# Retention and a gated MLP on one core: the first eight rows in whole chunks of 128 tokens, and loads that wait for the fourth in front

## The chip, the cores and the metric

The kernel runs on one core of a Trainium2 chip. The metric is device time in microseconds (us), as the median of several executions. A profile is one execution recorded by the hardware: it lists what TensorE (PE, with its weight loads as PEld), VectorE (DVE), ScalarE (ACT), GpSimd (POOL) and SyncE's DMA queue (SP) did, and when.

## What is computed

```python
def _attn_ref(q, k, v):                       # 4 batches, 8 heads, 768 tokens, 64 dims
    gamma = 1.0 - 2.0 ** (-5.0 - np.arange(H))
    for t in range(S):
        state = gamma * state + k[t] outer v[t]
        y[t] = q[t] @ state / sqrt(D)

def _moe_ref(x, w_in, w_out):                 # 3072 x 512, 512 x 2048, 2048 x 512
    h = x @ w_in
    g = h * clip(h + 3, 0, 6) / 6
    return g @ w_out
```

The retention's output, its heads side by side, is the x of the MLP. The weights come as 64-bit floats.

## The kernel before

**Rows and units.** A row is 128 tokens of one batch with all eight heads; there are 24. Row r is chunk n = r // 4 of batch r % 4, so four rows are the same chunk of the four batches. They make a unit of 512 tokens, of which there are six; `UR` is 4.

**Retention of a row.** The recurrence is worked in chunks. Before, each row is cut into two chunks of 64 tokens (c = 0 and 1). `decay` (L448) scales v by ScalarE (four heads) and GpSimd (four) in rows 0 to 3, by ScalarE alone in rows 4 to 7, by GpSimd alone later. `scores` (L361) multiplies k and q of each chunk, in 16 matmuls of 64x64 for the eight heads; `gather` (L385) multiplies k and v, which gives what the chunk adds to the state (16 more). VectorE masks the scores (`fading`, L499, into the tile am). `add_up` (L516) adds to the state of the chunk before: twice a row, on VectorE, or on ScalarE as a copy where there is no state yet. `outer_part` (L348) multiplies q with the state in front of the chunk, and `inner_part` (L373) v with the masked scores; both add in PSUM to y. VectorE scales y into xr (L572), and `split_step` (L241) makes a high part of it on ScalarE and the rest on VectorE: the tile x. `pace` (L343) is a tiny matmul that touches a bank of its own.

**The MLP.** `mm1_step` (L593) makes one h tile: 128 of the 2048 columns for the 512 tokens of a unit, 12 matmuls of 128x512 (L601), since x and w are each in two parts. ScalarE and VectorE make g from h, and SP stores it. `convert` (L182) makes 32-bit weights of a 64-bit tile: one load of 512 KB into one of two staging buffers (st), one step on ScalarE (wm), four on VectorE (wm, wb, wb, ww), and then the split. The second product (L787) runs when all of g is stored, in 1008 matmuls.

**What sets the order.** The program is written as steps, each with an engine, a cost, what it needs and a rank. `Plan.order` (L71) plays them through: TensorE's steps in the order of the code, the others by readiness and rank; the result is the order of each engine's instructions, which is then fixed. Only the numbers in `Plan` decide it; on the chip, each instruction waits for its semaphores in that order. Loads by SP are steps too. The table `FIRST` (L403) fixes the order of the first loads: vn of row 0, the first weight tile, kt, qt, kn, then vn, kt, qt, kn row by row with the tables dq and weight tiles between. All 32 loads of rows 0 to 7 go to the tiles "early". Later rows load into kt, qt, vn and kn; the plan lets such a load start after the third last h tile in the order of the code (L432). Loads are issued on eight semaphores in turn, so that each waits for the eighth DMA in front. Where the plan sees TensorE idle in its first 60 us, `spin` (L700) puts matmuls on constant data, whose results are not used.

Of the kernel before, what the change touches and what calls it, by code (L numbers as in the profile page):

```python
# [19 lines left out]
P = 128  # L20
# [21 lines left out]
class Plan:  # L42
# [3 lines left out]
    FIRST, RATE, FLIGHT = 2.0, 0.00266, 2.0  # L46
# [24 lines left out]
    def order(self):  # L71


        left = {}
        for n, step in enumerate(self.steps):
            step.n = n
            left.setdefault(step.engine, []).append(step)
        for step in self.steps:
            step.all = self.needs(step)
        free = dict.fromkeys(left, self.FIRST)  # L80
        dma = port = self.FIRST
        done = []
        while any(left.values()):
            best = None
            for engine, steps in left.items():
                ready = []
                line = steps[:1] if engine == "PE" else steps
                if engine == "SP" and min(x.rank for x in steps) < -50:
                    line = [min(steps, key=lambda x: x.rank)]
                for step in line:  # L90
                    if all(d.end is not None for d in step.all):
                        at = max([free[engine], port * step.port] + [d.end for d in step.all])
                        ready.append((at, step.rank, step.n, step))
                if ready:
                    t = min(ready)[0]
                    pick = min((r for r in ready if r[0] <= t + 1e-9), key=lambda r: r[1:3])
                    if best is None or t < best[0]:
                        best = (t, pick[3])
            t, step = best
            step.start, free[step.engine] = t, t + step.cost  # L100
            step.end = t + step.cost + step.seen
            if step.port:
                port = t + step.cost
            if step.kb:
                dma = max(dma, t + self.FLIGHT) + step.kb * self.RATE
                step.end = dma
            left[step.engine].remove(step)
            done.append(step)
        return sorted(done, key=lambda x: (x.start, x.n))
# [3 lines left out]
def retention_ffn(ctx: ExitStack, tc: tile.TileContext, qkv, w_in, w_out, dvs, dqs, out, B, H, S, D):  # L113
# [18 lines left out]
    SPIN, FILL = 60.0, 0.7  # L132
    AHEAD = 2 * UR
# [47 lines left out]

    def convert(src, rank, soon=None):  # L182
# [4 lines left out]
        def fetch():  # L187
            t["st"] = wst_tile("st", I64, 2)
            nc.sync.dma_start(out=t["st"], in_=src)
            words = t["st"].bitcast(I32).rearrange("p (n w) -> p n w", w=2)  # L190
            t["lo"], t["hi"] = words[:, :, 0], words[:, :, 1]
# [156 lines left out]
    def outer_part(t, n, states):  # L348

        for i, c, a, h in tiles:  # L350
            if n or c:
                nc.tensor.matmul(  # L352
                    t["y"][halves[a], h, i, cut[c]],
                    states[c][halves[h], a, i],
                    t["qt"]["t"][halves[h], 2 * i + a, cut[c]],
                    start=(i, c) == (0, int(not n)),
                    stop=False,
                    skip_group_check=True,
                )

    def scores(t):  # L361

        for i, c, a, h in tiles:
            nc.tensor.matmul(  # L364
                t["sc"][a][halves[h ^ a], i, c],
                t["kt"]["t"][halves[h], 2 * i + a, cut[c]],
                t["qt"]["t"][halves[h], 2 * i + a, cut[c]],
                start=True,
                stop=True,
                skip_group_check=True,  # L370
            )

    def inner_part(t):  # L373

        for i, c, a, h in tiles:
            nc.tensor.matmul(  # L376
                t["y"][halves[a], h, i, cut[c]],
                t["vn"]["t"][halves[h ^ a], 2 * i + a, cut[c]],
                t["am"][halves[h ^ a], a, i, c],
                start=False,  # L380
                stop=True,
                skip_group_check=True,
            )

    def gather(t, n):  # L385

        for i, c, a, h in tiles:
            if not c or n < ROWS_B - 1:
                nc.tensor.matmul(  # L389
                    t["u"][a][halves[h], c, i],  # L390
                    t["kn"]["t"][halves[h ^ a], 2 * i + a, cut[c]],
                    t["vn"]["t"][halves[h ^ a], 2 * i + a, cut[c]],
                    start=True,
                    stop=True,
                    skip_group_check=True,
                )
# [17 lines left out]
    def load_part(x, src, o, rank):  # L414
# [10 lines left out]
        def fetch():  # L425
# [4 lines left out]
            nc.sync.dma_start(out=to["t"].rearrange("p h n -> p (h n)"), in_=src)  # L430

        return to, box, add("SP", 0.35, fetch, tiles_done[-3:-2], rank, (box,), kb=256)  # L432

    def load(r, rank):
# [13 lines left out]
        def decay(pool, hs):  # L448
# [4 lines left out]
            else:  # L453
# [9 lines left out]
                rank + 3.5,  # L463
                (t["box", "vn"],),
            )
            for pool, hs, size in (((0, slice(0, 4), 4), (1, slice(4, 8), 4)) if r < UR else ((0, slice(0, 4), 4), (0, slice(4, 8), 4)) if r < AHEAD else ((1, slice(0, 8), 8),))
        ]

    def scores_step(r, at):
        t = rows[r]  # L470

        spare = r < UR and r % 2
        t["sc box"] = [plan.box("h", NH) for _ in range(2)] if spare else [plan.box("sc", 1)]

        def run():
# [5 lines left out]
            parts = [b.rearrange("p (b i c n) -> p b i c n", b=2, i=2, n=HALF) for b in banks]  # L481
            t["sc"], t["u"] = ([p[:, b] for p in parts] for b in range(2))
            t["banks"] = [(both, slice(0, 2))] if not spare else [(b[:, None], slice(a, a + 1)) for a, b in enumerate(banks)]
            scores(t)

        t["S"] = add("PE", 0.5, run, (t["got", "kt"], t["got", "qt"]), at, (*t["sc box"], t["box", "kt"], t["box", "qt"]))

    def gather_step(r, at):
        t, n = rows[r], r // UR
# [3 lines left out]
            lambda: gather(t, n),  # L493
# [4 lines left out]

        def fading():  # L499
            t["am"] = apool.tile([P, 2, 2, 2, HALF], F32, tag="am", name=nm("am"), bufs=1)  # L500
            for b, a in t["banks"]:
                nc.vector.tensor_tensor(
                    out=t["am"][:, a].rearrange("p a i c n -> p a (i c) n"),
                    in0=b[:, :, 0 : 2 * P].rearrange("p a (x n) -> p a x n", n=HALF),
                    in1=mask[:, None, None].to_broadcast([P, a.stop - a.start, 4, HALF]),
                    op=ALU.mult,
# [4 lines left out]
        t["A"] = add("DVE", 0.61 + more, fading, (t["S"], t["G"], t["masked"]), at + 2, (*t["sc box"], t["am box"]))  # L511
        t["adds"] = {}
        for c in range(2 if n < ROWS_B - 1 else 1):
            t["state box", c] = plan.box(f"state{c}", 2 + c * (UR - 1))

            def add_up(c=c):  # L516
                new = apool.tile([P, 2, 2, D], F32, tag=f"state{c}", name=nm("state"), bufs=2 + c * (UR - 1))
                was = rows[r - UR]["state", 1] if not c and n else t.get(("state", 0))
                for b, a in t["banks"]:
                    u = b[:, :, (2 + c) * P : (3 + c) * P]  # L520
                    to = new[:, a].rearrange("p a i n -> p a (i n)")
                    if n or c:
                        nc.vector.tensor_tensor(  # L523
                            out=to, in0=u, in1=was[:, a].rearrange("p a i n -> p a (i n)"), op=ALU.add
                        )
                    else:
                        nc.scalar.activation(out=to, in_=u, func=AF.Copy)
                t["state", c] = new
# [3 lines left out]
            if c:  # L532
                boxes.append(t["state box", 0])
                deps.append(t["adds"][0])
            elif n:
                boxes.append(rows[r - UR]["state box", 1])
                deps.append(rows[r - UR]["adds"][1])
            eng = ("DVE", 0.34 + more) if n or c else ("ACT", 0.37 + more)
            t["adds"][c] = add(*eng, add_up, deps, at + 1.5 + 2 * c, boxes)

    def outer_step(r, at):
        t, n = rows[r], r // UR
        t["y box"] = plan.box("y", 1)
        was = rows[r - UR] if n else None

        def run():
            ys = ps_a.tile([P, 2, UT], F32, tag="y", name=nm("y"))[:, :, 0 : 2 * P]
            t["ys"], t["y"] = ys, ys.rearrange("p h (i n) -> p h i n", i=2)
            outer_part(t, n, [was and was["state", 1], t["state", 0]])
            pace()  # L550

        states = [t["state box", 0]] + ([was["state box", 1]] if n else [])
        deps = [t["adds"][0], t["S"], was and was["adds"][1]]
        t["T"] = add("PE", 0.55 if n else 0.3, run, deps, at, (t["y box"], t["box", "qt"], *states))

    def inner_step(r, at):
        t, u = rows[r], r // UR
        n = u

        def run():  # L560
            pace()
            inner_part(t)

        t["I"] = add("PE", 0.55, run, (t["A"], t["T"]), at, (t["y box"], t["am box"], t["box", "vn"]))
# [64 lines left out]
    rows.update((r, {"masked": got_mask}) for r in range(NROW))  # L629
# [41 lines left out]
    for n, (u, jj) in enumerate(turns):  # L671
        while n_w1 < min(NF, jj + 2):
            build_w1(n_w1, next(at) + (0.5 if n_w1 == 0 else 2.0))
# [274 lines left out]
```

## Time and profile before

| | us |
|---|---|
| median of 3 runs (589.95 to 590.63) | 589.98 |
| the profiled execution | 588.12 |
| its span, first to last instruction | 586.3 |
| TensorE busy in the span | 569.6 |
| VectorE busy | 420.2 |
| ScalarE busy | 242.0 |

The profiled execution is 1.86 us below the median of the runs. The span opens with rows 0 to 3, goes on with h tiles between rows, and ends with the second product. Two things are to be kept in mind. Spins count as busy time of PE, and so do matmuls that wait in the pipe. And "issue" in the chain or among the waits is time in which an engine waited for nothing that the profile shows.

### The profile page before, as it was taken

The page shows a single profiled execution, that of the slowest core. Times are in us where ns is not written, and L with a number is a line of the kernel's source. Part 1 is how long each engine was busy: PE and PEld are TensorE (multiplying, and loading weights), DVE is VectorE, ACT ScalarE, POOL GpSimd, SP SyncE. Part 2 cuts the span into 40 slices and gives each one's busy share as a digit, 9 for nine tenths or more (in the row PEclk, how much of TensorE's full clock was granted, in tenths as well). Part 3 has the DMA queues.
Part 4 walks back from the last instruction along what each step waited for, and adds up shares of the span by engine and source line. Part 5 has one row for each costly group of instructions (what it writes and reads, how often), then busy time and mean ns, then how long its engine had stood idle before and what let it go on. Part 6 is the DMA issues. An engine that isn't in the chain of part 4 may idle for free.

```text
span 586.3 us, 13047 instructions
## 1 busy us (share of the span) xinstructions
PE 569.6 (97%) x5250; PEld 467.5 (80%) x5250; DVE 420.2 (72%) x762; ACT 242.0 (41%) x432; POOL 20.2 (3%) x25
## 2 busy tenths in 40 slices
PE   7699999999999999999999999999999999999997
PEld 6577888887888887888888888888888888888885
DVE  4388898998944696443345967998699966899653
ACT  5374444554422343222243544444444344354340
POOL 1000000000000100000000000000000000000000
PEclk9799999999999999999999999999999999999999
DMA  9855756866655566444445529974789536896002
GB/s 328 324 181 202 248 189 231 261 213 221 214 206 173 186 227 210 159 167 146 148 162 189 185 90 340 391 228 119 248 283 315 175 99 190 286 331 208 0 2 107
DMA packets 61260, 119.93 MB, mean 205 GB/s; under 512 B 7056, under 2 KB 7312, under 8 KB 61200
## 3 DMA queue, kind: packets, MB, share of 16 engines
q1 hardware_dynamic: 60912, 119.04, 60.2%
q8 instruction: 41, 0.67, 0.5%
q14 instruction: 19, 0.16, 0.1%
q10 hardware_dynamic: 288, 0.06, 0.0%
HBM read 87.61 MB, written 31.46 MB: 203 GB/s over the span
## 4 chain that ended last, share of the span: by engine, by line
PE 90%; DMA 4%; issue 2%; DVE 1%; POOL 1%; SPq 0%; ACT 0%; DVEq 0%; POOLq 0%
PE h L601 42%; PE o L787 40%; DMA vn<-in_qkv 3%; PE y L376 3%; PE sc L389 2%; PE sc L364 2%; DMA early<-in_qkv 2%; PE y L352 2%; POOL vn L452 1%; SPq L430 0%; DVE x L160 0%; DVE xr L572 0%; DVE w L160 0%; PE spin L703 0%; PE pace L346 0%
## 5 line engine op out<-in xcount | busy, mean ns | idle before, releaser
L601 PE MATMUL h<-x,w 128*128 128x512 f32 x1152 | 268.7, 392 | 1.5 <-DVE x L160 0.9
L601 PEld LDWEIGHTS h<-x,w 128*128 128x128 f32 x1152 | 214.5, 188 | 47.8 <-DVE x L160 1.3
L787 PE MATMUL o<-gc,w 128*128 128x512 f32 x1008 | 233.2, 393 | 0.0
L787 PEld LDWEIGHTS o<-gc,w 128*128 128x128 f32 x1008 | 189.3, 188 | 43.7
L610 DVE SCALAR_TENSOR_TENSOR g<-g,h 128x512 f32<-128x512 f32 x96 | 65.9, 686 | 84.1 <-ACT g L607 83.4
L607 ACT ACTIVATE g<-h,three 128x512 f32<-128x512 f32 x96 | 66.1, 688 | 131.1 <-PE h L601 130.7
L238 ACT ACTIVATE gc<-gr 128x512 fp32r<-128x512 f32 x120 | 71.4, 623 | 56.9 <-PE o L787 43.1
L160 DVE TENSOR_TENSOR gc<-gr,gc 128x512 fp32r<-128x512 f32 x120 | 79.4, 685 | 20.7 <-ACT gc L238 20.7
L238 ACT ACTIVATE gc<-keep 128x512 fp32r<-128x512 f32 x48 | 30.4, 632 | 64.5 <-PE o L787 42.2
L160 DVE TENSOR_TENSOR gc<-keep,gc 128x512 fp32r<-128x512 f32 x48 | 32.9, 687 | 14.0 <-ACT gc L238 13.9
L195 ACT ACTIVATE wm<-st 128x512 f32<-128x512 f32 x32 | 21.5, 671 | 22.7 <-DMA st<-in_w_out 12.5
L246 ACT ACTIVATE x<-xr 128x512 fp32r<-128x512 f32 x24 | 15.1, 629 | 32.4 <-DVE xr L572 32.3
L452 POOL TENSOR_TENSOR vn<-vn,cst_sb 128x512 f32<-128x512 f32 x16 | 17.4, 1090 | 253.0 <-DMA vn<-in_qkv 239.3
L804 DVE SCALAR_TENSOR_TENSOR u<-o,u 128x512 f32<-128x512 f32 (+1 forms) x31 | 20.1, 666 | 6.4 <-PE o L787 6.4
L220 DVE SCALAR_TENSOR_TENSOR ww<-st,wb 128x512 int32<-128x512 int32 x32 | 22.7, 710 | 0.4
L214 DVE SCALAR_TENSOR_TENSOR wb<-st,wb 128x512 int32<-128x512 int32 x32 | 22.0, 686 | 0.3
L160 DVE TENSOR_TENSOR w<-ww,w 128x384 fp32r<-128x384 f32 (+2 forms) x34 | 19.9, 591 | 1.1 <-ACT w L246 1.1
L246 ACT ACTIVATE w<-ww 128x384 fp32r<-128x384 f32 (+2 forms) x34 | 18.5, 550 | 4.6 <-DVE ww L220 4.5
L163 DVE TENSOR_TENSOR keep<-gr,gr 128x512 f32<-128x512 f32 x24 | 16.4, 688 | 4.8 <-DMA gr<-gd 4.5
L523 DVE TENSOR_TENSOR state<-sc,state 128x256 f32<-128x256 f32 (+1 forms) x42 | 16.9, 406 | 4.0 <-PE sc L389 3.7
L199 DVE TENSOR_SCALAR wm<-wm 128x512 f32<-128x512 f32 x32 | 13.5, 422 | 8.3 <-ACT wm L195 8.3
L160 DVE TENSOR_TENSOR x<-xr,x 128x512 fp32r<-128x512 f32 x24 | 16.4, 685 | 1.6 <-ACT x L246 0.9
(51 smaller groups left out, 340.6 us busy)
## 6 DMA issues: line engine op xcount, KB each, us to landing
gr<-gd SPq DMA_DIRECT2D x168, 256.0 KB, 4.1
gd<-g SPq DMA_DIRECT2D x96, 256.0 KB, 3.0
early<-in_qkv SPq DMA_DIRECT2D x32, 256.0 KB, 5.4
st<-in_w_in SPq DMA_DIRECT2D x16, 512.0 KB, 4.0
st<-in_w_out SPq DMA_DIRECT2D x16, 512.0 KB, 3.9
kt<-in_qkv SPq DMA_DIRECT2D x16, 256.0 KB, 3.3
qt<-in_qkv SPq DMA_DIRECT2D x16, 256.0 KB, 3.8
vn<-in_qkv SPq DMA_DIRECT2D x16, 256.0 KB, 4.4
```

The costliest lines, as they stand in the source:

```text
L160: return nc.vector.tensor_tensor(out=out_, in0=a, in1=b, op=ALU.subtract)
L195: nc.scalar.activation(out=t["m"], in_=t["hi"].bitcast(F32), func=AF.Abs)
L214: nc.vector.scalar_tensor_tensor(out=b, in0=t["hi"], scalar=-0x40000000, in1=b, op0=ALU.bitwise_and, op1=ALU.bitwise_or)
L220: nc.vector.scalar_tensor_tensor(out=t["w"].bitcast(I32), in0=t["lo"], scalar=29, in1=t["b"], op0=ALU.logical_shift_right, op1=ALU.bitwise_or,
L238: nc.scalar.activation(out=hi, in_=src, func=AF.Copy)
L246: nc.scalar.activation(out=hi, in_=src, func=AF.Copy)
L452: nc.gpsimd.tensor_tensor(out=v, in0=v, in1=scale[:, :, None].to_broadcast([P, hs.stop - hs.start, D]), op=ALU.mult)
L601: nc.tensor.matmul(h, w[:, o, a], xs[u][b][:, k], start=k + n == 0, stop=(k, n) == (NK - 1, 2), skip_group_check=True)
L607: nc.scalar.activation(out=t["g"], in_=t["h"], func=AF.Relu, bias=three)
L610: ins = nc.vector.scalar_tensor_tensor(out=t["g"], in0=t["g"], scalar=6.0, in1=t["h"], op0=ALU.min, op1=ALU.mult)
L787: nc.tensor.matmul(banks[b, i, h], w2c[jj][:, RIGHT[i], a, h], gc[:, q, c], start=jj == 0 and n == 0, stop=jj == NFP - 1 and n == 2, skip_ ...
L804: nc.vector.scalar_tensor_tensor(out=out_[:, cut], in0=banks[b, i, h][:, cut], scalar=f, in1=other[:, cut], op0=ALU.mult, op1=ALU.add)
```

## The change

**Whole chunks.** The first eight rows (`wide`, r < 8) are one chunk of 128 tokens. Of the 128x128 scores of a head three blocks of 64x64 are needed: two on the diagonal, and one with the keys of the first half and the queries of the second. Scores and inner part take the first half of the keys against all 128 queries (a matmul of 64x128) and the second half against its own (64x64). VectorE still masks the two diagonal blocks; the block off the diagonal is copied to am by ScalarE (`passing`). The two halves of k and v add up in PSUM, so that a row has one state, added once. The outer part takes 128 queries at once against one state, and rows 0 to 3 have none. Rows 8 to 23 stay in chunks of 64.

```diff
-    def outer_part(t, n, states):
+    def outer_part(t, n, states, wide):
         for i, c, a, h in tiles:
-            if n or c:
+            if (n or c) and not (c and wide):
                 nc.tensor.matmul(
-                    t["y"][halves[a], h, i, cut[c]],
+                    t["y"][halves[a], h, i, whole_or_cut(c, wide)],
...
     def gather(t, n, wide):
...
-                    start=True,
-                    stop=True,
+                    start=not wide or (i, c) == (0, 0),
+                    stop=not wide or c == 1,
...
+        def passing():
+            am = am_tile()
+            for b, a in t["banks"]:
+                nc.scalar.activation(
+                    out=am[:, a, :, HALF:P],
+                    in_=b.rearrange("p a (i x n) -> p a i x n", i=2, n=HALF)[:, :, :, 1],
+                    func=AF.Copy,
+                )
...
+        if wide:
+            t["A"].append(add("ACT", 0.37 + more, passing, deps, at + 2, (*t["sc box"], t["am box"])))
...
         for c in range(2 if n < ROWS_B - 1 else 1):
+            if wide and not c:
+                continue
```

**Loads.** Every load of q, k, v, dq and of weights goes through one function that adds a wait for the fourth such load in front; the plan has the same rule. Loads of later rows may be planned two h tiles sooner. The third and fourth weight tiles stand one row earlier in the table of first loads.

```diff
+    def load_from(to, src):
+        ins = nc.sync.dma_start(out=to, in_=src).ins
+        if len(started) >= plan.DEPTH:
+            tc.add_manual_dep(ins, started[-plan.DEPTH], behind, reason="few loads at a time")
+        started.append(ins.name)
...
-        FIRST += {1: [(0, "dq")], 3: [("w", 1)], 4: [(1, "dq")], 5: [("w", 2)], 6: [("w", 3)], 7: [("w", 4)]}.get(r, [])
+    BEHIND = {1: [(0, "dq")], 3: [("w", 1)], 4: [(1, "dq"), ("w", 2)], 5: [("w", 3)], 7: [("w", 4)]}
...
-        return to, box, add("SP", 0.35, fetch, tiles_done[-3:-2], rank, (box,), kb=256)
+        return to, box, add("SP", 0.35, fetch, tiles_done[-5:-4], rank, (box,), kb=256)
```

`FADE`, `W_FIRST`, `W_NEXT` name ranks; FADE is 4.5 where it was 3.5, so the plan takes decays a little later. The first eight rows share out the decays as before.

**What it does to the order.** TensorE, the third row (r = 2). sc is the PSUM tile of its scores and gathered state, y that of the row in front; the tiles early hold the loads. Before:

```order
L364 MATMUL sc_296<-early_125 64x64 x16
L352 MATMUL y_317<-early_118,state_279 64x64 x8
L346 MATMUL pace_326<-mask 64x4
L389 MATMUL sc_296<-early_125 64x64 x16
L346 MATMUL pace_344<-mask 64x4
L376 MATMUL y_317<-am_291,early_125 64x64 x16
```

After, at the same place:

```order
L383 MATMUL sc_267<-early_130 64x128 x4
L383 MATMUL sc_267<-early_130 64x64 x4
L383 MATMUL sc_267<-early_130 64x128 x4
L383 MATMUL sc_267<-early_130 64x64 x4
L408 MATMUL sc_267<-early_130 64x64 x16
L395 MATMUL y_305<-am_262,early_130 64x128 x4
L395 MATMUL y_305<-am_262,early_130 64x64 x4
```

The outer part and both pace matmuls are gone; half of the scores' matmuls, and of the inner part's, are 128 columns wide.

SP's queue from the second dq table on, with what each load waits for (DMAHW is the semaphore of a DMA in front; st is a weight tile). Before:

```order
L430 DMA early_143<-in_decays_y 128x512 [waits DMAHW1_49]
L430 DMA early_200<-in_qkv 128x512 [waits DMAHW2_49]
L430 DMA early_200<-in_qkv 128x512 [waits DMAHW3_49]
L430 DMA early_200<-in_qkv 128x512 [waits DMAHW4_49]
L430 DMA early_200<-in_qkv 128x512 [waits DMAHW5_49]
L189 DMA st_282<-in_w_in 128x512 [waits DMAHW6_49,DVE_49,Activation_49]
```

After:

```order
L189 DMA early_257<-in_decays_y 128x512 [waits DMAHW5_49]
L189 DMA st_411<-in_w_in 128x512 [waits DMAHW6_49,DVE_49,Activation_49]
L189 DMA early_400<-in_qkv 128x512 [waits DMAHW7_49]
L189 DMA early_400<-in_qkv 128x512 [waits DMAHW0_49]
L189 DMA early_400<-in_qkv 128x512 [waits DMAHW1_49]
L189 DMA early_400<-in_qkv 128x512 [waits DMAHW2_49]
L189 DMA st_461<-in_w_in 128x512 [waits DMAHW3_49,DVE_49,Activation_49]
```

The third weight tile moved from behind the four loads of row 5 to ahead of them, and the fourth to right behind them; the semaphores stand for the fourth load in front instead of the eighth.

VectorE, from the masks of the fourth row (am) to the end of its x; wm, wb and ww are steps of the second weight tile. Before:

```order
L502 TENSOR_TENSOR am_449<-sc_374,mask 128x256
L523 TENSOR_TENSOR state_467<-sc_373,state_442 128x128
L523 TENSOR_TENSOR state_467<-sc_374,state_442 128x128
L199 TENSOR_SCALAR wm_445<-wm_445 128x512
L572 TENSOR_TENSOR xr_495<-y_456,early_143 128x512
L160 TENSOR_TENSOR x_294<-xr_447,x_294 128x4x128
L203 TENSOR_SCALAR wb_503<-wm_445 128x512
L214 SCALAR_TENSOR_TENSOR wb_503<-st_186,wb_503 128x512
L160 TENSOR_TENSOR x_294<-xr_495,x_294 128x4x128
```

After:

```order
L542 TENSOR_TENSOR am_404<-sc_335,mask 128x2x2x64
L214 TENSOR_SCALAR wm_398<-wm_398 128x512
L165 TENSOR_TENSOR x_265<-xr_402,x_265 128x4x128
L218 TENSOR_SCALAR wb_442<-wm_398 128x512
L633 TENSOR_TENSOR xr_449<-y_414,early_257 128x512
L229 SCALAR_TENSOR_TENSOR wb_442<-st_327,wb_442 128x512
L235 SCALAR_TENSOR_TENSOR ww_454<-st_327,wb_442 128x512
L165 TENSOR_TENSOR x_265<-xr_449,x_265 128x4x128
```

The additions of the state are gone, and two steps of the weight tile stand between the fourth row's xr and the end of its x, where before there stood a short and a long one, and the x of the third row.

More of the change, by code (lines that the diff above doesn't have):

```diff
@@ L91, in order @@
                     if all(d.end is not None for d in step.all):
-                        at = max([free[engine], port * step.port] + [d.end for d in step.all])
+                        at = max([landed[-self.DEPTH]] if step.kb and len(landed) >= self.DEPTH else [0.0])
+                        at = max([at, free[engine], port * step.port] + [d.end for d in step.all])
                         ready.append((at, step.rank, step.n, step))
@@ L359, in outer_part, with scores @@
                 )
-    def scores(t):
+    def scores(t, wide):
         for i, c, a, h in tiles:
             nc.tensor.matmul(
-                t["sc"][a][halves[h ^ a], i, c],
+                t["sc"](a, i, c)[halves[h ^ a]],
                 t["kt"]["t"][halves[h], 2 * i + a, cut[c]],
-                t["qt"]["t"][halves[h], 2 * i + a, cut[c]],
+                t["qt"]["t"][halves[h], 2 * i + a, whole_or_cut(c, wide)],
                 start=True,
@@ L371, in scores, with inner_part @@
             )
-    def inner_part(t):
+    def inner_part(t, n, wide):
         for i, c, a, h in tiles:
             nc.tensor.matmul(
-                t["y"][halves[a], h, i, cut[c]],
+                t["y"][halves[a], h, i, whole_or_cut(c, wide)],
                 t["vn"]["t"][halves[h ^ a], 2 * i + a, cut[c]],
-                t["am"][halves[h ^ a], a, i, c],
-                start=False,
+                t["masked"](a, i, c)[halves[h ^ a]],
+                start=wide and not n and (i, c) == (0, 0),
                 stop=True,
@@ L383, in inner_part, with gather @@
             )
-    def gather(t, n):
+    def gather(t, n, wide):
         for i, c, a, h in tiles:
@@ L470, in scores_step @@
         t = rows[r]
-        spare = r < UR and r % 2
+        spare, wide = r < UR and r % 2, r < AHEAD
         t["sc box"] = [plan.box("h", NH) for _ in range(2)] if spare else [plan.box("sc", 1)]
@@ L492, in gather_step @@
             0.5 if n < ROWS_B - 1 else 0.25,
-            lambda: gather(t, n),
+            lambda: gather(t, n, wide),
             (*t["faded"], t["got", "kn"]),
@@ L531, in gather_step @@
             deps = [t["G"]]
[L532 to L538, printed above, removed]
+            if before:
+                boxes.append(before["state box", k])
+                deps.append(before["adds"][k])
+            eng = ("ACT", 0.37 + more) if first_ else ("DVE", 0.34 + more)
@@ L539, in gather_step, with y_tile @@
             t["adds"][c] = add(*eng, add_up, deps, at + 1.5 + 2 * c, boxes)
+    def y_tile(t):
+        ys = ps_a.tile([P, 2, UT], F32, tag="y", name=nm("y"))[:, :, 0 : 2 * P]
+        t["ys"], t["y"] = ys, ys.rearrange("p h (i n) -> p h i n", i=2)
     def outer_step(r, at):
-        t, n = rows[r], r // UR
-        t["y box"] = plan.box("y", 1)
+        t, n, wide = rows[r], r // UR, r < AHEAD
+        t["y box"], t["T"] = plan.box("y", 1), None
+        if wide and not n:
+            return
@@ L544, in outer_step @@
         was = rows[r - UR] if n else None
         def run():
-            ys = ps_a.tile([P, 2, UT], F32, tag="y", name=nm("y"))[:, :, 0 : 2 * P]
-            t["ys"], t["y"] = ys, ys.rearrange("p h (i n) -> p h i n", i=2)
-            outer_part(t, n, [was and was["state", 1], t["state", 0]])
+            y_tile(t)
+            outer_part(t, n, [was and was["state", 1], None if wide else t["state", 0]], wide)
             pace()
-        states = [t["state box", 0]] + ([was["state box", 1]] if n else [])
@@ L553, in outer_step @@
-        deps = [t["adds"][0], t["S"], was and was["adds"][1]]
-        t["T"] = add("PE", 0.55 if n else 0.3, run, deps, at, (t["y box"], t["box", "qt"], *states))
+        states = ([] if wide else [t["state box", 0]]) + ([was["state box", 1]] if n else [])
+        deps = [None if wide else t["adds"][0], t["S"], was and was["adds"][1]]
+        t["T"] = add("PE", 0.55, run, deps, at, (t["y box"], t["box", "qt"], *states))
     def inner_step(r, at):
-        t, u = rows[r], r // UR
+        t, u, wide = rows[r], r // UR, r < AHEAD
@@ L558, in inner_step @@
         n = u
         def run():
-            pace()
-            inner_part(t)
-        t["I"] = add("PE", 0.55, run, (t["A"], t["T"]), at, (t["y box"], t["am box"], t["box", "vn"]))
+            if t["T"]:
+                pace()
+            else:
+                y_tile(t)
+            inner_part(t, n, wide)
+        t["I"] = add("PE", 0.7 if wide else 0.55, run, (*t["A"], t["T"]), at, (t["y box"], t["am box"], t["box", "vn"]))
         if r % UR == 0:
@@ L627, in retention_ffn @@
     got_mask = add("ACT", 0.1, lambda: nc.scalar.dma_start(out=mask, in_=dvs[:, ROWS_B * H :]), (), -9.0)
-    rows.update((r, {"masked": got_mask}) for r in range(NROW))
+    rows.update((r, {"got mask": got_mask}) for r in range(NROW))
     at = iter(range(1 << 30))
@@ L672, in retention_ffn @@
         while n_w1 < min(NF, jj + 2):
-            build_w1(n_w1, next(at) + (0.5 if n_w1 == 0 else 2.0))
+            build_w1(n_w1, next(at) + (W_NEXT if n_w1 else W_FIRST))
             n_w1 += 1
```

88 lines of the change are left out of this document (60 added, 28 removed).

## The prediction

> **What bounds the kernel now.** I read four views in this order: the page's engine row, busy time in four stretches that I cut myself, the chain that ended last, and TensorE's waits. First the page and the stretches; each stretch's row is length, then busy time of PE, PEld, DVE, ACT and POOL with counts, the granted clock, the DMA share and GB/s.
>
> ```profile
> PE 569.6 (97%) x5250; PEld 467.5 (80%) x5250; DVE 420.2 (72%) x762; ACT 242.0 (41%) x432; POOL 20.2 (3%) x25
> ...
> 0.00:31.83 31.83, 21.83 (x508) 18.70 (x508) 13.98 (x30) 15.01 (x47) 2.76 (x9) 0.89 0.82 301
> 31.83:56.52 24.69, 23.74 (x584) 19.10 (x584) 20.77 (x42) 13.28 (x34) 1.16 (x1) 1.00 0.66 225
> 56.52:349.66 293.14, 291.01 (x3153) 240.73 (x3154) 198.56 (x388) 113.77 (x182) 16.28 (x15) 1.00 0.57 191
> 349.66:586.30 236.64, 233.01 (x1008) 188.99 (x1007) 186.93 (x304) 100.00 (x171) 0.00 (x0) 1.00 0.63 206
> ```
>
> PE is full from 56.52 us on: 2.1 us idle in 293, and in the last stretch, which the change does not touch, only the tail. So the change can pay in the first 56.52 us and in those 2.1 us, nowhere else. The cuts are pieces of the chain (start, length, what):
>
> ```profile
> 13.45 2.27 issue
> ...
> 19.43 2.52 issue
> ...
> 26.88 1.29 issue
> ...
> 31.83 2.83 PE h L601 x11
> ...
> 38.70 0.62 PE sc L364 x32
> 39.32 0.47 PE y L352 x32
> ...
> 40.36 0.58 PE y L376 x29
> ...
> 45.39 0.52 PE sc L389 x29
> ...
> 56.52 5.70 PE h L601 x24
> ```
>
> At 31.83 the first full tile of the first product (h) starts, once four rows of attention have given x; from 56.52 on its tiles run back to back. The three "issue" pieces ahead of 31.83 are 6.08 us in which PE waited for no semaphore. TensorE's waits name them, and a second, small wait:
>
> ```profile
> PE sc L364 <- issue: 4.8, 2, 2.5
> PE y L376 <- issue: 1.6, 2, 1.3
> ...
> PE sc L389 <- POOL vn L452: 1.6, 4, 0.6
> ```
>
> What PE waits for without a semaphore, the DMA view suggests. Its queue rows read packets, MB, share; the first is of the whole span, the next three of single microseconds from 13, 25 and 29 us on.
>
> ```profile
> q8 instruction: 41, 0.67, 0.5%
> ```
>
> ```profile
> q8 instruction: 1, 0.02, 7.0%
> ```
>
> ```profile
> q8 instruction: 1, 0.02, 6.7%
> ```
>
> ```profile
> q8 instruction: 1, 0.02, 8.2%
> ```
>
> 41 packets against the 10,500 PE and PEld instructions of the page make 256 instructions a packet: q8 carries PE's program. A packet moves between 13 and 14 us and PE stands from 13.45 to 15.72; one moves between 25 and 26 and PE stands from 26.88 to 28.17. So I read the pieces as PE out of program, waiting for a block that came late behind the loads. How long the loads' line is, their own landing times show: the first load alone, the four of 0 to 3 us, the four of 12 to 15 us.
>
> ```profile
> early<-in_qkv SPq DMA_DIRECT2D x1, 256.0 KB, 3.0
> ```
>
> ```profile
> early<-in_qkv SPq DMA_DIRECT2D x4, 256.0 KB, 4.5
> ```
>
> ```profile
> early<-in_qkv SPq DMA_DIRECT2D x4, 256.0 KB, 7.0
> ```
>
> With eight in flight (before, each load waits for the eighth DMA in front) a load needs 7.0 us instead of 3.0. A block that stands in the same line comes some 4 us late.
>
> The Trainium skill says otherwise in two places. "Runtime: NRT & Kernel Launch", section "Instruction fetch mechanics", puts a block at 256 instructions, which the packets above confirm, and calls the crossing of a block "mostly hidden", which 6.08 us of standing PE contradict. "DMA: Bandwidth & Descriptors", section "Queues, rings and completion order", says that a DMA engine turns between its queues after each packet; by that rule fewer loads in flight would not bring the block sooner. No row shows when a block was asked for, so the rule stays open; it is the first rival below.
>
> **The change, part by part.**
>
> *Up to the first h tile (31.83 us).* Two limits count: the loads and the chain behind the last of them. The rows:
>
> ```profile
> 10.00:20.00 10.00, 6.49 (x250) 5.73 (x240) 4.09 (x10) 4.06 (x14) 1.23 (x2) 0.83 1.06 394
> 20.00:30.00 10.00, 6.71 (x157) 5.52 (x158) 4.54 (x11) 4.28 (x14) 0.00 (x0) 0.83 0.72 265
> ```
>
> ```profile
> 14.38 0.61 POOL L452 TENSOR_TENSOR early<-early,cst_sb 128x256 f32<-128x256 f32 x1 [2.07 <-DMA early<-in_qkv]
> ```
>
> ```profile
> 30.08 2.00 ACT L455 ACTIVATE early<-early,cst_sb 128x64 f32<-128x64 f32 x8
> ```
>
> Loads: at 394 GB/s, 256 KB take 0.67 us. Row 3's vn has landed at 14.38, its kn is three loads later: 16.4. With four in flight, four loads (1.05 MB) come in each 3.0 us and 0.1 of waking SP, 0.77 us a load, against 0.67 now; from kn of row 0, the fifth load, to kn of row 3 are 13 loads, so 1.3 us more: kn lands at 17.7. With 4.5 us of landing it would be 1.15 a load and 22.6; with no loss 16.4. I take 3.0, since the 4.5 row had a 512 KB load in its line.
>
> Behind kn of row 3 stand, with durations from the chain and from these groups of 0 to 57 us by form (busy us, mean ns):
>
> ```profile
> L572 DVE TENSOR_TENSOR xr<-y,early 128x512 f32<-128x512 f32 x8 | 5.5, 690 | 12.3 <-PE y L376 12.3
> ...
> L160 DVE TENSOR_TENSOR x<-xr,x 128x512 fp32r<-128x512 f32 x7 | 4.8, 682 | 0.0
> L246 ACT ACTIVATE x<-xr 128x512 fp32r<-128x512 f32 x7 | 4.4, 625 | 7.1 <-DVE xr L572 7.1
> ...
> L523 DVE TENSOR_TENSOR state<-sc,state 128x256 f32<-128x256 f32 x10 | 4.2, 417 | 0.0
> L502 DVE TENSOR_TENSOR am<-sc,mask 128x512 f32<-128x512 f32 x6 | 4.1, 683 | 1.0 <-PE sc L389 1.0
> ...
> L527 ACT ACTIVATE state<-sc 128x256 f32<-128x256 f32 x2 | 0.7, 374 | 2.6 <-PE sc L389 2.6
> ```
>
> gather 0.52, row 2's xr 0.69 and the mask 0.68 on VectorE, the inner part 0.58 and up to half more for its wide matmuls (0.8), xr 0.69, x high 0.63, x low 0.68: 4.7 us. Two queues lengthen it. ScalarE has row 4's eight decays (2.00) ahead of x high, part of which falls into the time before xr; VectorE has two operations of a weight conversion ahead of x low. I add 1.2. The end is 17.7 + 4.7 + 1.2 = 23.6. The program may be late once more. The three pieces end at 15.72, 21.95 and 28.17, 6.2 us apart; if a block is asked for when the former begins to run, it takes 6.2 us now. Counted on by 256 instructions from the first piece, the next block but one begins in row 3's gather, asked for after row 2's scores, at some 13.5. At 6.2 us it costs PE 2 more there, at 4 nothing; I add 0.7: **24.3**, 7.5 us earlier. Bounds: 22.5 (no loss on the loads, block in time) and 27 (twice the load loss, the block at 6.2 us, the rest for the order of the queues). That the stalls and the half-clock stretches (0.83 in the mean in both windows) make 7.5 us possible at all is checked from the other side: 6.08 us of stalls, and rows 0 to 3 lose outer parts (half of 0.47 each, as only one chunk has a state in front) and pace matmuls that waited for them. The off-diagonal copy on ScalarE (0.37 a row, by the state copy of the same 256 columns) lies beside VectorE's mask of 0.68, so it costs nothing as long as ScalarE is free; if not, 0.37 each.
>
> *From the first h tile to the full PE (24.69 us).* VectorE was 20.77 us busy here and drops one state addition in each of rows 4 to 7: 4 × 0.42 = 1.7. ScalarE gains 4 × 0.37 = 1.5 on 13.28. PE: 4 h tiles of 2.85 (two ran in 5.70) and four rows of 0.62 + 0.47 + 0.52 + 0.58 = 2.19 are 20.2 us; the other 4.5 are waits, mostly for VectorE (spins fill part of them, and count as busy). Scores and inner part now have half their matmuls 128 columns wide: between nothing and half of 0.62 + 0.58 more per row, 0.6. The outer part has half as many, each twice as wide: nothing. No row shows a 64x128 matmul; I take the middle, 0.3 a row, so PE needs 21.4. Of the waits I let half stay, since VectorE loses only 1.7 of 20.77: 23.6, **1.1 us less**. Bounds 21.4 (no wait left) and 26 (all waits, the wide matmuls at their dearest). The loads of the third and fourth weight tiles move ahead by a row; they still wait for one of two staging buffers, and four qkv loads stand behind each on SP's queue. These were not what PE waited for, so nothing.
>
> *From 56.52 us on.* Loads of a row of attention are planned two h tiles (5.7 us) sooner. Four waits for vn's decay on GpSimd make 1.6 us, 0.6 at most each; 5.7 us cover them: **1.6 us less**, bounds 0 and 1.6. The wait for the fourth load stands on SP's queue ahead of stores of g, but loads come four at a time and land in 3 to 6 us between tiles of 2.85, so a store is seldom held, and g has three buffers: nothing.
>
> Sum: 7.5 + 1.1 + 1.6 = 10.2 us. The profiled execution took 588.12 us (span 586.3), so 577.9 in its terms; the median of the runs shown is 589.98, 1.86 above it, so **579.8** in theirs.
>
> **Rivals.**
>
> 1. *The stalls stay* (the page's rule, or a wait that does not bind because the loads are spaced anyway). For it: the skill's rule, and that no request is seen. Against: three late blocks while loads flow, and landing times that double with the line. Two blocks instead of three end before the first h tile (rows 0 to 3 lose a sixth of their matmuls), each late by up to 2.4 us, of which 0.7 is counted: 3.5 us back, 583.3.
> 2. *Rows 4 to 7 become ScalarE's.* Each copy stands in order behind eight decays of 2.00 us, and the inner part waits for it. For: four masks of rows 4 to 7 each have such decays near. Against: ScalarE is only 13.28 of 24.69 us busy. At 1 us a row, 4 us, and the 1.1 lost: 584.9.
> 3. *Four loads starve the queue: slower.* If landing keeps 5.4 us with four in flight, the median of the page's row:
>
> ```profile
> early<-in_qkv SPq DMA_DIRECT2D x32, 256.0 KB, 5.4
> ```
>
> then 1.05 MB come in 5.5 us, 1.38 a load instead of 0.67. kn of row 3 comes 9.2 us later, at 25.6, first h tile at 31.5 to 32; some 16 more loads of rows 4 to 7 and weights end 20 us late in all, and the second stretch waits 3 us: 591.5. It decides from about 1.3 us a load on, where the gain of the first stretch is gone. Against: the first load alone took 3.0.
> 4. *No change*: gains and losses cancel, 589.98.
>
> **How the numbers follow.** Forecast 0.61, rival 1 0.15, rival 2 0.12, rival 3 0.08, rival 4 0.04. Forecast, 1 and 2 are faster: 0.88; 0.04 same; 0.08 slower (0.2%, or 1.2 us, is about what a measurement of this kernel can tell from no change). The best bounds together (22.5, 21.4, 1.6) give 14.2 us, the worst (27, 26, 0) 3.5: 575.8 to 586.5. I take 576 to 586.5, which holds rivals 1 and 2 and leaves out 3 and 4.
>
> **What would show it.** Right: no "issue" piece over 1 us in the chain before the first h tile; that tile at 22.5 to 27 us; landing of qkv loads near 3 us in the first 20 us; h tiles back to back from about 47.9; no wait of PE for GpSimd. Wrong: "issue" pieces of 2 us (rival 1), PE waiting for ScalarE's am in rows 4 to 7 (rival 2), GB/s near 200 in 10 to 20 us and PE waiting for loads (rival 3).

## The result, and the profile after

| | before | changed |
|---|---|---|
| median of 22 runs, us | 590.41 (587.78 to 594.71) | 587.45 (585.25 to 590.52) |
| ratio | 1 | 0.9950, 95% interval 0.9935 to 0.9965 |
| profiled execution, us | 588.12 | 588.53 |
| its span | 586.3 | 586.7 |

The change gains 3.0 us of the 10.2 that were forecast, and 587.45 lies above the range of 576 to 586.5. The profiled execution of before lies below its median and that of the changed kernel above its own, so the two traces tell where time moved, and the medians how much is gained.

Busy time of the changed kernel in the same four stretches as before, cut at the first full h tile, at the point from which h tiles run back to back, and at the second product (length, then PE, PEld, DVE, ACT, POOL, clock, DMA share, GB/s):

```profile
0.00:29.21 29.21, 20.16 (x429) 17.89 (x429) 13.25 (x24) 14.80 (x45) 2.76 (x9) 0.94 0.80 259
29.21:59.27 30.06, 24.45 (x513) 19.89 (x513) 21.85 (x40) 16.59 (x45) 1.58 (x2) 0.97 0.80 269
59.27:350.07 290.80, 290.74 (x3157) 240.95 (x3154) 197.30 (x384) 112.77 (x181) 16.61 (x15) 1.00 0.56 191
350.07:586.70 236.63, 233.02 (x1009) 188.95 (x1007) 186.52 (x304) 99.93 (x171) 0.00 (x0) 1.00 0.63 206
```

Against before the first stretch is 2.6 us shorter (forecast 7.5), the second 5.4 longer (forecast 1.1 shorter), the third 2.3 shorter (forecast 1.6), the last the same. The chain that ended last says what took the place of the stalls (start, length, what):

```profile
8.89 4.14 DMA early<-in_qkv
13.05 4.54 DMA early<-in_qkv
17.60 6.12 DMA st<-in_w_in
23.74 3.06 DMA early<-in_qkv
26.82 6.28 DMA early<-in_qkv
33.12 4.79 DMA early<-in_qkv
37.92 3.12 DMA early<-in_qkv
41.11 5.05 DMA st<-in_w_in
...
52.17 3.81 DMA st<-in_w_in
```

Up to 46 us the chain is nearly nothing but loads that follow one another: each starts when one in front has landed. Before, loads stood there up to 13 us only, and "issue" and PE behind them. TensorE's waits of the changed kernel have no "issue" in them any more; the longest are:

```profile
PE sc L383 <- DMA early<-in_qkv: 4.6, 2, 2.6
PE sc L383 <- ACT x L261: 2.5, 1, 2.5
PE y L395 <- DVE am L542: 1.6, 2, 1.3
```

and the wait for vn's decay on GpSimd is gone as well. ScalarE's longest wait in the second stretch is for weight tiles:

```profile
ACT wm L210 <- DMA st<-in_w_in: 12.4, 5, 3.9
```

Before, no wait for such a load stands among ScalarE's waits of this stretch.

What the loads do, SP's queue shows: eight loads of 256 KB each, before in 5.27 us,

```profile
6.02 5.27 SPq L430 DMA_DIRECT2D early<-in_qkv  x8
```

and in the changed kernel in 8.39, a load each 1.05 us instead of 0.66.

```profile
8.89 8.39 SPq L189 DMA_DIRECT2D early<-in_qkv  x8
```

The last of them, kn of row 3, is what that row's gather waits for, until 21.78 us:

```profile
21.78 0.69 PE L408 MATMUL sc<-early 64*64 64x64 f32 x32 [1.03 <-DMA early<-in_qkv]
```

The stretch from 10 to 20 us of the changed kernel moves 256 GB/s, where it was 394:

```profile
10.00:20.00 10.00, 6.23 (x202) 5.82 (x206) 2.75 (x6) 3.99 (x14) 1.23 (x2) 0.84 0.80 256
```

### The profile page after: what moved, and what is told of

Same layout as the page of the kernel before. It is cut to its first block, busy times and chain, and to the rows that moved or that the text cites. A ratio compares the mean times of both kernels' runs of the same rounds, so it can differ in the third digit from the quotient of the medians.

```text
span 586.7 us, 12760 instructions
## 1 busy us (share of the span) xinstructions
PE 568.4 (97%) x5102; PEld 467.7 (80%) x5102; DVE 418.9 (71%) x752; ACT 244.1 (42%) x442; POOL 20.9 (4%) x25
## 4 chain that ended last, share of the span: by engine, by line
PE 90%; DMA 8%; DVE 1%; ACT 0%; issue 0%; SPq 0%; DVEq 0%; ACTq 0%
PE h L662 44%; PE o L848 40%; DMA early<-in_qkv 6%; DMA st<-in_w_in 3%; PE y L395 2%; PE sc L383 2%; PE y L371 1%; PE sc L408 1%; SPq L189 0%; ACT wm L210 0%; DVE am L542 0%; DVE wb L229 0%; ACT g L668 0%; ACT w L261 0%; DVE ww L235 0%
## 5 line engine op out<-in xcount | busy, mean ns | idle before, releaser
L253 ACT ACTIVATE gc<-keep 128x512 fp32r<-128x512 f32 x48 | 30.4, 632 | 64.4 <-PE o L848 42.2
L261 ACT ACTIVATE x<-xr 128x512 fp32r<-128x512 f32 x24 | 15.1, 630 | 27.2 <-DVE xr L633 27.1
L229 DVE SCALAR_TENSOR_TENSOR wb<-st,wb 128x512 int32<-128x512 int32 x32 | 23.3, 727 | 0.2
L168 DVE TENSOR_TENSOR keep<-gr,gr 128x512 f32<-128x512 f32 x24 | 16.4, 686 | 5.8 <-DMA gr<-gd 5.7
L542 DVE TENSOR_TENSOR am<-sc,mask 128x512 f32<-128x512 f32 (+1 forms) x26 | 16.5, 641 | 3.4 <-ACT am L547 2.2
```

What stands on the lines that cost most here:

```text
L229: nc.vector.scalar_tensor_tensor(out=b, in0=t["hi"], scalar=-0x40000000, in1=b, op0=ALU.bitwise_and, op1=ALU.bitwise_or)
L253: nc.scalar.activation(out=hi, in_=src, func=AF.Copy)
L261: nc.scalar.activation(out=hi, in_=src, func=AF.Copy)
```

## The experiments

Two theories stood against each other. A: the wait for the fourth load takes the stalls away but slows the loads by more than it saves. B: the wait is where the gain comes from. Ratios below are to the kernel before on the same chip in the same session.

| kernel | loads in flight | ratio, 95% interval | median, us | GB/s, 10 to 20 us | first full h tile | h back to back from |
|---|---|---|---|---|---|---|
| before | 8 | 1 | 590.41 | 394 | 31.83 | 56.5 |
| changed | 4 | 0.9950 (0.9935 to 0.9965) | 587.45 | 256 | 29.21 | 59.3 |
| e6_wait5 | 5 | 0.9859 (0.9837 to 0.9881) | 581.87 | 307 | 27.76 | 52.5 |
| e2_wait6 | 6 | 0.9855 (0.9827 to 0.9883) | 580.73 | 344 | 26.98 | 50.5 |
| e1_no_wait | 8 | 0.9892 (0.9872 to 0.9913) | 583.02 | 393 | 28.39 | 54.8 |

### The changed kernel without the wait, and with five and six in flight

```diff
-        if len(started) >= plan.DEPTH:
-            tc.add_manual_dep(ins, started[-plan.DEPTH], behind, reason="few loads at a time")
```

> The changed kernel without the wait for the fourth load in front; the order on every engine is the same, and each load again waits for the eighth DMA in front. Theory A (the wait cures the late program blocks but slows the loads by more than it saves): 10 to 20 us moves over 380 GB/s again instead of 256, qkv loads land in 5 to 7 us, one or two issue pieces of 2 us or more come back before the first h tile, that tile still starts earlier than the 29.2 us of the changed kernel (25 to 27), PE is full from 52 to 55 instead of 59.3, and the time is 582 to 585 against 587.45. Theory B (the wait is where the gain comes from, the slower loads are a small price): issue pieces come back, first h tile at 30 or later, time 589 to 591.

Measured: 583.02 us, as theory A had it. The rate is back and so are the stops of PE. Rows of TensorE's timeline without the wait, each the first work after a stop:

```profile
16.19 0.33 PE L381 MATMUL sc<-early 64*64 64x64 f32 x3 [2.54 <-issue]
...
22.22 0.28 PE L406 MATMUL sc<-early 64*64 64x64 f32 x3 [1.99 <-issue]
```

The first h tile comes at 28.4, later than the 25 to 27 expected of A, but earlier than in the changed kernel.

So whole chunks, the new places of the loads and the sooner loads are worth 1.1% or 6.4 us by themselves (0.9892), and the wait for the fourth takes 3.4 of these back (0.9950 less 0.9892). Of the three, the sooner loads were also run alone (below); whole chunks and the new places were not run apart.

```diff
-        if len(started) >= plan.DEPTH:
-            tc.add_manual_dep(ins, started[-plan.DEPTH], behind, reason="few loads at a time")
+        if len(started) >= 6:
+            tc.add_manual_dep(ins, started[-6], behind, reason="few loads at a time")
```

> The changed kernel with the wait for the sixth load in front instead of the fourth, order the same. Theory A: rate in 10 to 20 us between 256 and 390 GB/s, at least 330; issue pieces of at most 1 us; first h tile at 25 to 27 us; time 582 to 585, as good as without the wait or a little better. Theory B: 587 to 590, between the changed kernel and the one without the wait.

Measured: 580.73, better than A had it. The first two stretches of this kernel, cut at the same events, and the start of the second product in its chain:

```profile
0.00:26.98 26.98, 21.20 (x430) 18.20 (x430) 13.26 (x25) 16.02 (x48) 2.88 (x9) 0.94 0.90 315
26.98:50.51 23.53, 23.08 (x514) 19.22 (x514) 21.55 (x39) 15.72 (x44) 2.63 (x2) 1.00 0.85 304
...
342.19 233.03 PE o L848 x1008
```

The program on every engine is that of the changed kernel, and only the number in the wait differs. The second stretch is 23.53 us long, where the prediction had 23.6 and the changed kernel 30.06. ScalarE's wait for weight tiles in it has shrunk from 12.4 us:

```profile
ACT wm L210 <- DMA st<-in_w_in: 3.5, 3, 1.8
```

The granted clock does not make the difference to four in flight: it was 0.94 in the first stretch of both, and 1.00 against 0.97 in the second, which is worth 0.9 us of 30.06 at most (an estimate from these two rows). The "issue" expected at 1 us at most was 1.8 in one place, so six in flight does not cure all of it.

With five in place of six:

```diff
+        if len(started) >= 5:
+            tc.add_manual_dep(ins, started[-5], behind, reason="few loads at a time")
```

> The changed kernel with the wait for the fifth load in front, order the same. Rate of 10 to 20 us between 256 (fourth) and 344 GB/s (sixth): about 300; first h tile at 27.5 to 28.5; time 582 to 585. If the fourth is a point where the rate breaks off, rather than one on a slope, it is level with the sixth: 580 to 581.5.

Measured: 581.87, between the two ranges that were expected and level with six by its ratio, though its rate, 307 GB/s, is on the slope. So the time breaks off between five and four; the rate does not. The break lies in the second stretch, 24.8 us with five and 30.1 with four by the table; ScalarE waits 5.3 us for weight tiles in it with five, 12.4 with four. Why one load makes so much there is not shown.

### The parts on the kernel before

The function `load_from` is brought into the kernel before, and its loads go through it; the lines below show the wait alone.

```diff
...
+        if len(started) >= 4:
+            tc.add_manual_dep(ins, started[-4], behind, reason="few loads at a time")
```

> The kernel before with nothing but the wait for the fourth load in front, order the same as before. Theory A: issue pieces of 2 us vanish, but the rate in 10 to 20 us falls to 260 to 300 GB/s and PE waits for loads instead; first h tile at 30 to 33 us, time within 2 us of the kernel before (589 to 592.5). Theory B: most of the gain of the whole change is here, 587 to 588.5.

Measured: 592.59 us, ratio 1.0048 (1.0025 to 1.0070): slower, and at the upper end of what A had. Theory B falls. TensorE's waits now begin with loads:

```profile
PE sc L374 <- DMA early<-in_qkv: 4.7, 3, 2.7
PE y L386 <- issue: 2.9, 2, 2.0
PE sc L374 <- issue: 2.3, 1, 2.3
```

The stops did not vanish altogether, as theory A had expected: none of 2 us is left before the first h tile, at 29.23, but one of 2.32 stands behind the first two tiles, at 36.07.

With six in place of four:

```diff
...
+        if len(started) >= 6:
+            tc.add_manual_dep(ins, started[-6], behind, reason="few loads at a time")
```

> The kernel before with nothing but the wait for the sixth load in front. If whole chunks and the wait each give their own part (the wait of six 2.3 us, by the changed kernel with and without it): 587.5 to 588.5. If the wait pays only together with whole chunks, because the old chain of row to row hides it: 589.5 to 591. If the wait gives most: 583 to 585.

Measured: 587.71, ratio 0.9961 (0.9942 to 0.9980). A wait of six gives 2.3 us on the kernel before (1.2 to 3.4 by the interval) and about 2.2 on the changed one (0.9892 less 0.9855, whose intervals overlap a little): as far as these can tell, a part of its own, whatever the chunks. It also shows how far apart blocks of program come. The first work after three stops:

```profile
14.56 0.52 PE L374 MATMUL sc<-early 64*64 64x64 f32 x21 [0.65 <-issue]
...
20.06 0.39 PE L374 MATMUL sc<-early,early 64*64 64x64 f32 x11 [2.68 <-issue]
...
25.86 0.93 PE L386 MATMUL y<-am,early 64*64 64x64 f32 x25 [0.92 <-issue]
```

The blocks arrive 5.5 and 5.8 us apart, with eight in flight 6.2 (the ends of the stops in the profile of before). Two loads fewer go with some 0.6 us less from block to block. In the profiles of the other kernels of this document the first blocks came 4.9 and 5.7 us apart with six in flight (e2_wait6, e8_plan6) and 6.0 to 6.5 with eight (e1_no_wait, e4_old_far, e5_more_program).

```diff
-        return to, box, add("SP", 0.35, fetch, tiles_done[-3:-2], rank, (box,), kb=256)
+        return to, box, add("SP", 0.35, fetch, tiles_done[-5:-4], rank, (box,), kb=256)
```

> The kernel before with nothing but later rows' loads planned two h tiles sooner. If the 1.6 us of waits for vn's decay on GpSimd were worth what I counted: those waits gone, time 1.0 to 1.6 us below the kernel before (588.8 to 589.4). Rival: the loads come sooner but collide with weight loads or stores, or the waits are hidden elsewhere: no change within 0.5 us.

Measured: 588.39, ratio 0.9971 (0.9950 to 0.9992), 1.7 us with an interval of 0.5 to 2.9, a little more than expected. GpSimd is no longer among TensorE's waits. This term of the prediction holds.

### What the stops are

```diff
...
+    for n in range(16):
+        nc.tensor.matmul(idle[0:64, 0:4], warm[0:64, 0, 0:64], warm[0:64, 1, 0:4], start=True, stop=True)
```

> The changed kernel without the wait, and 16 tiny matmuls (64x4, on constant data, result unused) behind the warm-up: 64 more instructions of PE ahead of everything else. Without them PE stood after 29 of the 32 records of row 2's scores and after 27 of the 32 records of row 3's gather. If PE stands because a block of 256 instructions has not come, both places move 64 instructions (32 records) back: the first stop falls in row 0's inner part (y, about one record before its end), the second in row 3's scores, after some 27 of 32 records. If PE stands for data, a buffer or the clock, the stops stay at row 2's scores and row 3's gather.

Rows of TensorE's timeline, two pairs of the work before and after a stop:

```profile
12.62 0.85 PE L395 MATMUL y<-am,early 64*64 64x128 f32 x31
15.99 0.21 PE L395 MATMUL y<-am,early 64*64 64x64 f32 x1 [2.52 <-issue]
...
18.70 0.84 PE L383 MATMUL sc<-early,early 64*64 64x128 f32 x27
22.43 0.34 PE L383 MATMUL sc<-early,early 64*64 64x64 f32 x5 [2.90 <-issue]
```

Both stops moved as expected, to the record: PE now stands one record before the end of the inner part, and after 27 of 32 records of the scores. Whatever the data, the stop is at a fixed number of instructions. The "issue" pieces are PE out of program: 2.52 and 2.90 us at these two blocks. The Trainium skill calls the crossing of a block "mostly hidden" ("Runtime: NRT & Kernel Launch", section "Instruction fetch mechanics"); this trace does not agree. The kernel ran once (581.14 us), so nothing is read from its time.

The packets of PE's program say how a block is held up. In the kernel before, the stops end at 15.72, 21.95 and 28.17 us, and the next packets start at 19.47, 25.81 and 29.22. The first and the last of these stretches, from the end of a stop to the next packet:

```profile
15.72:19.47 3.75, 3.71 (x127) 3.52 (x126) 0.42 (x1) 0.39 (x1) 0.00 (x0) 0.54 1.04 390
...
28.17:29.22 1.05, 1.05 (x28) 0.93 (x28) 0.40 (x1) 0.00 (x0) 0.00 (x0) 1.00 0.08 16
```

While loads flow at 390 GB/s, the packet starts 3.75 us after PE has entered the new block (3.86 in the second case); when hardly anything else moves, it starts after 1.05 us, in which PE has run no more than 28 matmul records of the block. So the packet comes late while loads flow, if it is asked for when PE enters the block in front; when it is asked for, no row shows.

### How slow four in flight are, and where that hurts

> The changed kernel with the wait for the second load in front: measures landing with two in flight. If landing is a fixed 3.0 us until the engines are full (what the prediction took from the first load): 1.5 to 1.6 us from load to load, about 170 GB/s. If a load among others lands in some 4.2 us however few they are: 2.1 to 2.2 us a load, about 125 GB/s. Time 600 us or more either way, first h tile beyond 38 us.

```diff
+        if len(started) >= 2:
+            tc.add_manual_dep(ins, started[-2], behind, reason="few loads at a time")
```

Measured, in one run: 620.8 us, first h tile at 38.59. The landing time and SP's queue with two in flight:

```profile
early<-in_qkv SPq DMA_DIRECT2D x16, 256.0 KB, 2.9
```

```profile
15.21 12.88 SPq L189 DMA_DIRECT2D early<-in_qkv  x8
```

A load lands in 2.9 us and they follow each other in 1.61. So 3.0 us is right for one load, and for two. The changed kernel's row of the first 30 us, with four:

```profile
early<-in_qkv SPq DMA_DIRECT2D x23, 256.0 KB, 4.4
```

Landing has grown with four (three were not run), long before the rate is full: 163 GB/s with two, 256 with four, 307 with five, 344 with six, 394 with eight.

```diff
-        if len(started) >= plan.DEPTH:
+        if plan.DEPTH <= len(started) < 18:
```

> The changed kernel with the wait for the fourth load in front on the first 18 loads only (rows 0 to 3, their dq table and the first weight tile); order the same. Theory A (slow loads late in the start, above all of weight tiles and rows 4 to 7, lengthen the second stretch): first h tile near the 29.2 us of the changed kernel, at 28.5 to 29.5, then full PE within 23 to 25 us of it instead of 30; time 581.5 to 584. Rival: the second stretch is long because of the wide matmuls and ScalarE's copies, whatever the loads do: 28 us or more again, time 586 to 588.

Measured: 582.60, ratio 0.9873 (0.9851 to 0.9896). The first full tile and the start of those that run back to back:

```profile
30.43 2.79 PE L662 MATMUL h<-x,w 128*128 128x512 f32 x11 [0.35 <-DVE x L165]
...
54.88 5.75 PE L662 MATMUL h<-x,w 128*128 128x512 f32 x24
```

The first stretch is as slow as in the changed kernel (30.4, above the 28.5 to 29.5 expected), the second is 24.45 us instead of 30.06. The rival, wide matmuls and ScalarE's copies, would have left it long. ScalarE waits 0.8 us for weight tiles in it, where it was 12.4. So the wait on loads from the 19th on costs the larger part. The time is even that of the kernel without any wait (583.02, 0.9892) within the intervals: on the first 18 loads the wait takes the stops away and seems to lose about as much by slower loads. One profile tells no more than this of the first stretch, since the eight loads of rows 2 and 3 start at 10.33 us here and at 8.89 in the changed kernel, though up to there the two wait alike.

### Better versions

In the first, the plan knows the wait of six, too:

```diff
-    FIRST, RATE, FLIGHT, DEPTH = 2.0, 0.00266, 2.0, 4
+    FIRST, RATE, FLIGHT, DEPTH = 2.0, 0.00266, 2.0, 6
```

> The changed kernel with the wait for the sixth load in front, and the plan knowing it, so that the order follows (a few places on SP and VectorE move). Within 1 us of the sixth on the chip alone (580.7): 579.8 to 581.7. If the plan's order at four was part of the loss: 578 to 579.7.

Measured: 580.01, ratio 0.9824 (0.9802 to 0.9846). It has the lowest median of all, 10.4 us below the kernel before. Against the wait of six on the chip alone the intervals overlap. A stop of 2.6 us for a late block still stands ahead of its first h tile, at 27.00.

In the second, the wait of the first is on 18 loads only:

```diff
-        if len(started) >= plan.DEPTH:
+        if plan.DEPTH <= len(started) < 18:
```

> The wait for the sixth load in front, known to the plan, on the first 18 loads only; eight in flight from then on. If the remaining loss to the wait is in the second stretch: 578 to 579.5, below the 580.0 with the wait on all loads. If PE's late blocks come back there: 580.5 to 582.

Measured: 582.50, ratio 0.9876 (0.9852 to 0.9900), worse, and just above what was expected if late blocks come back. Late blocks do not explain it: they make 1.8 and 1.7 us in the first 60 us, but 2.6 and 0.6 in the version above. PE waits 2.8 us for loads, where it was 0.9, and the first h tile is at 30.04, where it was 27.00. Why the start is slower, though its 18 loads wait as in the version above, was not settled; in the profiled executions the load of the first dq table was already 1.6 us later (8.51 against 6.91), ahead of any load on which the two differ.

## Why the prediction was wrong

**The bound of the kernel was read rightly.** The time moved in the first 59 us and in the stretch behind them, and the second product took the same. The stretch behind gave a little more than the 2.1 us of idle that the prediction saw in it: 2.3 in the changed kernel, and 3.2 in the fastest one (51.44 to 341.34 us). That "issue" is missing program is shown by the stops that moved with 64 instructions.

**The step that failed is the time of a load: "four loads (1.05 MB) come in each 3.0 us and 0.1 of waking SP, 0.77 us a load".** It measured 1.05 (the waking of SP is 0.02 of it, from 8.89 and 4.14 to the next load at 13.05 in the chain). The 3.0 us were those of a load alone. The row of 4.5 us for the first four stood in the same part and would have given 1.15, nearer than what I took; I set it aside for its 512 KB load. The run with two in flight shows that 3.0 holds there and no further. From kn of row 0 to kn of row 3 the 0.28 us a load make 3.6 us. In the trace row 3's gather started at 21.78, 4.1 us behind the 17.7 of the prediction, and 0.9 of these lie in the base: before, kn of row 3 was issued at 10.96 and landed 6.3 us later, at 17.3 and not at the 16.4 that was counted on from vn. The rest of the 4.9 us that the first h tile was late is the chain behind, 7.4 us for the 6.6 forecast. With 1.15 a load the prediction's own sum would have come to 29.2 us, the time measured, but in part by luck, with the early base and the short chain in it. The bound of 27 us for the first h tile was too tight for the same reason: it took twice the small loss and not the one that the 4.5 row gives.

**Its consequence for the second stretch was put at nothing.** There I wrote of the loads "These were not what PE waited for, so nothing". With 1.05 us a load they became just that: ScalarE waited 12.4 us for weight tiles, and the stretch grew to 30.06. Taking the wait off the loads from the 19th on brought 24.45 back. This is the larger half of what was missed: in the profiles h tiles run back to back 11.4 us later than forecast (59.3 against 47.9), 4.9 of it from the first stretch and 6.5 from the second.

**The third rival was the mechanism, at a lower price.** It had four loads in 5.5 us, 1.38 a load, and slower than before; its point of decision, 1.3 a load, agrees with a change that still gains at 1.05, but no run tests it. Its chance of 0.08 was too small: the rows of 5.4 and 4.5 us of landing both spoke for slower loads.

**The range was narrower than its own terms.** The bound of 26 us for the second stretch was to hold all waits and the wide matmuls at their dearest; 20.2, 4.5 and four times 0.6 make 27.1. With it the range would have ended at 587.6 and held the measured 587.45. That would have been luck: the stretch took 30.06, beyond this bound too, by a wait that the prediction had ruled out. In rival 1, two blocks of 2.4 us less 0.7 make 4.1 us and not 3.5.

**The other terms held once the loads keep up.** With six in flight and the same program the second stretch is 23.53 (forecast 23.6), the third 291.7 (from 50.51 to 342.19, 1.5 us less; forecast 1.6), and only the first is 2.7 us above 24.3, just inside its bounds. The sooner loads alone gave 1.7 us. Wide scores and inner part cost a little more than reckoned, as the chain of e2_wait6 shows in a row behind an h tile:

```profile
39.58 0.83 PE sc L383 x32
...
41.43 0.81 PE y L395 x18
```

That is 0.83 instead of 0.62 and 0.81 instead of 0.58, some 0.4 us a row where 0.3 was reckoned. The second rival, ScalarE's copies, is ruled out for the second stretch by the same 23.53.

**That a block comes sooner when fewer loads are in flight** is borne out in its direction. With six in flight the blocks came 4.9 to 5.8 us apart, with eight 6.0 to 6.5, so there is an effect, smaller than the 2 us I had for four. With four in the changed kernel no block was late, but the loads gave them time as well; in the kernel before, four left stops of 2.3 and 2.0 us behind the first h tile. The prediction had read this against the rule that a DMA engine turns between its queues after each packet (the Trainium skill, "DMA: Bandwidth & Descriptors", section "Queues, rings and completion order"). The late packets above speak against a block that passes the loads without delay, but when a block is asked for, no row shows, so the rule is neither kept nor broken by these runs.

## What to carry to other kernels

How many loads may be in flight is a trade between the rate and the delay of everything else in the same engines: measure the rate at each number before choosing, since a load alone tells nothing of four. A wait that is put on all loads for the sake of the first ones also falls on those that come later and that another engine waits for. And where a wait is one part of a larger change, the change without it should be run: here one part took away half of what the others gave.

## What was not expected of the hardware

Loads of 256 KB on one queue keep each other waiting long before the rate is full: landing 2.9 us with two in flight, 4.4 with four, some 6 to 7 with eight, while the rate goes from 163 to 256 to 394 GB/s. With four in flight the share of the DMA engines was 0.80, three quarters of the 1.06 with eight, and the rate 0.65 of it; why was not tried. And TensorE can run out of program: without the wait it used up a block between 16.19 and 20.23 us (the end of the second stop less its 1.99), in 4.0, while blocks came 6.0 apart (16.19 and 22.22).
